# Two-layer-MLP pair behind sparse attention: chunk 0 of the first MLP in program order, eight weight buffers, W_out spilled as one float32 tensor, softmax over eight groups per operation

## The chip, the cores and the metric

The kernel runs on one core of one Trainium2 chip. The metric is the device time of one execution in microseconds (us). Before the change it is 860.85 us, the median of three runs (857.78 to 861.45).

## What is computed

Float64 inputs: q, k, v of shape (4, 8, 576, 64) and four weight matrices. Heads 0 to 3 see a local window of 32 positions, heads 4 to 7 see every 32nd position. The attention output is reshaped to 2304 tokens of 512 and goes through two MLPs with a hidden width of 2048, with different activations.

```python
scores = scale * np.matmul(q, k.transpose(0, 1, 3, 2))
scores = np.where(masks[None, :, :, :], scores, -1000000000.0)
attn = softmax(scores)
x = np.matmul(attn, v)            # then reshaped to (2304, 512)
h = x @ moe_w_in
g = h * np.clip(h + 3.0, 0.0, 6.0) / 6.0
x = g @ moe_w_out
h = x @ moe2_w_in
g = np.maximum(h, 0.0) + np.log1p(np.exp(-np.abs(h)))
return g @ moe2_w_out
```

## The kernel before

**Arithmetic.** Every float32 matrix product is made of three products of a high and a low part (hi x hi, hi x lo, lo x hi; a part is of type fp32r). So a tensor is "split" before TensorE uses it: ScalarE (ACT) copies it to the high part, VectorE (DVE) subtracts that to get the low part. The weights arrive as 64-bit words and are first turned into float32: `w_scale` on ACT changes the upper word in place, then `w_bits` on DVE makes one operation on the lower word (TENSOR_SCALAR, line 121) and one that joins both (SCALAR_TENSOR_TENSOR, line 127).

**Stages.** A prologue computes the attention of the first 96 positions of each batch element, which give chunk 0 (384 tokens). Chunks 1 to 4 are the other 480 tokens of each of the four batch elements. The first MLP walks over chunks, and in each over 16 blocks `f` of 128 hidden columns; one such pair is a *slot*, n = 16 c + f. In a slot TensorE (PE) makes the first product of block f (`pe_h`, 12 matmuls into one of two PSUM banks `psh`) and the second product of the block two slots earlier (`pe_y`, 12 matmuls). Between them stand `post1` (ACT adds 3 and clips, DVE makes the clip at 6 and the product: tile `r`), `post2a` (ACT: high part `gh`) and `post2b` (DVE: low part `gl`). The second MLP follows with its own scheme and is not touched, but its weights are prepared (`prep`) in the slots from chunk 1 on.

**Attention beside the first MLP.** The attention of the tokens of chunk c + 1 is computed in the slots of chunk c. A table `fill`, filled by `put(half-slot, function)`, says in which half-slot each step stands: transposes, `a_qk` (scores into PSUM), `a_max`, `a_exp`, `a_rec`, `a_pt` (transposes), `a_pv`, `a_px`. In `a_max` one fused DVE operation per group of 36 or 64 columns adds the mask and takes the row maximum; `a_exp` is one ACT operation per group, with the sum as an accumulator. There are 16 groups for each kind of head.

**Weights of the first MLP.** In chunk 0 the blocks of W_in and W_out are loaded (512 KB each, DMA issued by SP, five buffers), converted and split. The parts of W_in stay in SBUF for all chunks (`wih`, `wil`). The two parts of W_out (`woh`, `wol`) live in a ring of twelve buffers, are written to DRAM by POOL's queue (`wdr`, two times 256 KB a block) and loaded again four slots ahead in every later chunk (`load_split`).

**Order.** Each engine runs its instructions in the order in which they stand in its program. From chunk 1 on, `in_order` (line 848) makes this the order in which the code is written. In the prologue and in chunk 0 a scheduler in the compiler orders the instructions by its own estimate of when each can start; `after(...)` only keeps some of them behind a few marked ones. The slots of chunk 0 are written in `slot` (line 1244), the prologue is lines 1118 to 1240.

Of the kernel before, what the change touches and what calls it, by code (L numbers as in the profile page):

```python
# [16 lines left out]
P = 128  # L17
# [5 lines left out]
def attn_two_mlps(  # L23
# [51 lines left out]
    ps_a = ctx.enter_context(tc.tile_pool(name="ps_a", bufs=1, space=bass.MemoryType.PSUM))  # L75
# [13 lines left out]
    wdr = [dram.tile([2, P, DM], F32, name=f"wdr{f}") for f in range(NF)]  # L89
# [8 lines left out]
    def load_win(l, f):  # L98
        t = wsl.tile([P, DM], I64, tag="w64", name="wi64", bufs=5)
        nc.sync.dma_start(out=t, in_=w_in[l][f].rearrange("p k f -> p (k f)"))  # L100
        wst_t[0, l, f] = t

    def load_wout(l, f):
        t = wsl.tile([P, DM], I64, tag="w64", name="wo64", bufs=5)
        nc.sync.dma_start(out=t, in_=w_out[l][f * P : (f + 1) * P, :])
        wst_t[1, l, f] = t

# [22 lines left out]

    def split_win(l, f):
        raw = words(0, l, f, F32)[1]
        wst_t.pop((0, l, f))
        hi = wp.tile([P, KT, P], F32R, tag="wih", name="wih")
        lo = wp.tile([P, KT, P], F32R, tag="wil", name="wil")
        wi_t[l, f] = (hi, lo)
# [4 lines left out]
    def sw_tile(name):  # L141
        return sw.tile([P, DM], F32R, tag="sw", name=name)

    def split_wout(f):
        raw = words(1, 0, f, F32)[1]
        wst_t.pop((1, 0, f))
        hi, lo = sw_tile("woh"), sw_tile("wol")
        nc.scalar.copy(hi, raw)
        nc.vector.tensor_tensor(out=lo, in0=raw, in1=hi.bitcast(F32), op=ALU.subtract)
        for i, t in enumerate((hi, lo)):  # L150
            nc.gpsimd.dma_start(out=wdr[f][i], in_=t.bitcast(F32))  # L151
        wo_t[0, f] = (hi, lo)

    def load_split(c, f):
        wo_t[c, f] = tuple(sw_tile(n) for n in ("woh", "wol"))
        for i, t in enumerate(wo_t[c, f]):
            nc.sync.dma_start(out=t.bitcast(F32), in_=wdr[f][i])
# [60 lines left out]
    def prep(k):  # L218
# [7 lines left out]
        if h < 2:  # L226
            w_scale(o, 1, 2 * g + h)
            w_bits((o, 1, 2 * g + h))
# [32 lines left out]
    def ps_two(name):  # L261
        return ps_a.tile([P, 2, 512], F32, tag="a", name=name)

    def ps_att(name):

        x = spare.pop(0)
        if not isinstance(x, tuple):
            return x
        pool, tag = x
        if pool is ps_a:  # L270
            t = ps_two(name)
            spare.insert(0, t[:, 1])
            return t[:, 0]
# [295 lines left out]
    def s_trans(b, n, last=False):  # L569
# [16 lines left out]
        for pr in range(NP):  # L586
# [3 lines left out]
            nc.scalar.copy(u[n + "T"][:, o0 : o0 + end], ps[:, pr, :end])  # L590
# [5 lines left out]
    def a_qk(st, b):  # L596
        ps = ps_two("pss")
        w = KWIN[st]
        for pr in range(NP):
            u = un[st, b, pr]  # L600
            q, k = (u["q"], u["k"]) if st else (u["qT"], u["kT"])
            for g, i, m in blocks(st):
                o = (pr * NG + g) * w
                k0 = (BL if st else w) * m
                for e in range(2):
                    es = slice(e * D, (e + 1) * D)
                    nc.tensor.matmul(
                        ps[i * BL : (i + 1) * BL, e, o : o + w],
# [12 lines left out]
    def a_max(st, b, pr):  # L621

        w = KWIN[st]
        for e in range(2):
            for g in range(NG):
                o = (pr * NG + g) * w
                nc.vector.tensor_tensor_reduce(
                    out=sc_t[st][:, pr, g, e, :w],
                    in0=sc_ps[st, b][:, e, o : o + w],
                    in1=bmask[:, st * KWIN[0] : st * KWIN[0] + w],  # L630
                    scale=-SCALE,
                    scalar=3.0e38,
                    op0=ALU.add,
                    op1=ALU.min,
                    accum_out=stat[st, b][0][:, pr, g, e : e + 1],
                )

    def a_exp(st, b, pr, e):
        nm, sm = stat[st, b]
        for g in range(NG):  # L640
            s = sc_t[st][:, pr, g, e, : KWIN[st]]
            nc.scalar.activation(
                out=s, in_=s, func=AF.Exp, scale=-1.0,
                bias=nm[:, pr, g, e : e + 1], accum_out=sm[:, pr, g, e : e + 1],
            )
# [6 lines left out]
    def a_pt(st, b):  # L652
# [3 lines left out]
        for pr in range(NP):  # L656
            for g in range(NG):
                nc.tensor.transpose(
                    ps[:, pr, g * P : (g + 1) * P],
# [3 lines left out]
        for pr in range(NP):  # L663
            nc.scalar.copy(pt[:, pr], ps[:, pr])
        pt_t[st, b] = pt

    def a_pv(st, b):
# [4 lines left out]
        for pr in range(NP):  # L672
            u = un.pop((st, b, pr))
            for g, i, m in blocks(st):
                for e in range(2):
# [3 lines left out]
                        ps[i * BL : (i + 1) * BL, e, o : o + D],  # L679
# [772 lines left out]
```

## Time and profile before

| | |
|---|---|
| three runs, median (lowest to highest) | 860.85 us (857.78 to 861.45) |
| the profiled execution, its own time | 862.52 us |
| its span in the profile | 860.7 us |
| mean granted TensorE clock in it | 0.989 |
| TensorE matmuls busy | 823.3 us, 96% |
| chunk 0 of the first MLP, first to last matmul of its own | 30.5 to 133.1 us |

How to read it: the profile shows one execution, microsecond by microsecond, from the start of its span. PE is busy nearly all the time, but its busy time counts overlapping, pipelined matmuls, so a stretch in which PE is "busy" is not always one in which it runs at its peak; the start times of its matmuls tell that. Of the 40 slices of the page, PE is below 9 tenths only in the first two, the fifth and the last.

### The profile page before, as it was taken

What the parts mean: (1) busy time and instruction counts of PE and PEld (TensorE: products, weight loads), DVE (VectorE), ACT (ScalarE), POOL (GpSimd) and SP (SyncE); (2) the same over time, 40 slices, a digit from 0 to 9 for tenths busy, and PEclk for the clock granted to TensorE, in tenths of its full rate; (3) what the DMA queues carried; (4) which work ended last, traced back from release to release, by engine and by line L of the source; (5) the groups of instructions that cost most, each with busy time, mean ns of one, the idle gap of its engine ahead of it and who ended that gap; (6) DMA issues with size and microseconds to landing.
All of it is one profiled execution on the core that took longest, in us unless ns stands there. A gap on an engine that the chain in (4) does not pass through costs nothing.

```text
span 860.7 us, 17133 instructions
## 1 busy us (share of the span) xinstructions
PE 823.3 (96%) x6245; PEld 759.9 (88%) x6245; DVE 610.9 (71%) x1231; ACT 484.2 (56%) x978; POOL 80.3 (9%) x133
## 2 busy tenths in 40 slices
PE   4799899999999999999999999999999999999996
PEld 2598888888888888878888899999999999999996
DVE  5596875466865676667677748798677898587784
ACT  4488663564456445664555467853377844478530
POOL 3021121011211112011301100000000000000000
PEclk9799999999999999999999999999999999999998
DMA  8598997499878998776878598777899787997874
GB/s 247 131 381 225 305 324 256 149 205 327 315 270 242 282 297 298 240 237 234 303 269 311 205 353 285 243 249 248 250 289 341 238 249 220 300 306 245 249 247 111
DMA packets 170532, 225.46 MB, mean 262 GB/s; under 512 B 76432, under 2 KB 91664, under 8 KB 170448
## 3 DMA queue, kind: packets, MB, share of 16 engines
q1 hardware_dynamic: 156608, 180.90, 68.4%
q0 software_dynamic: 12032, 42.47, 13.0%
q10 hardware_dynamic: 1808, 0.98, 0.5%
q8 instruction: 50, 0.82, 0.4%
q14 instruction: 34, 0.28, 0.1%
HBM read 177.08 MB, written 47.19 MB: 261 GB/s over the span
## 4 chain that ended last, share of the span: by engine, by line
issue 40%; PE 38%; POOL 7%; DVE 6%; DMA 4%; ACT 4%; SPq 0%; POOLq 0%; DVEq 0%; ACTq 0%
PE psn L1038 15%; PE psm L894 11%; PE psa L1038 6%; POOL sdr L213 5%; PE psh L737 3%; PE psy L781 2%; DVE gq L876 2%; DVE gq L907 2%; DMA wi<-in_w_in_dram 1%; ACT r L913 1%; ACT r L942 1%; ACT r L912 1%; POOL wdr L151 1%; POOL ydr L792 1%; DMA lq<-in_ql_dram 1%
## 5 line engine op out<-in xcount | busy, mean ns | idle before, releaser
L894 PE MATMUL psm<-xh,su 128*128 128x384 f32 x672 | 172.2, 335 | 3.5 <-DVE u L876 3.5
L894 PEld LDWEIGHTS psm<-xh,su 128*128 128x128 f32 x672 | 121.5, 188 | 4.8 <-DVE u L876 4.8
L737 PE MATMUL psh<-xl,wih 128*128 128x480 f32 (+1 forms) x320 | 120.0, 375 | 5.2 <-DVE xl L246 5.2
L1038 PE MATMUL psn<-th,su 128*128 128x384 f32 x480 | 124.6, 339 | 0.0
L781 PE MATMUL psy<-gl,woh 128*128 128x480 f32 (+1 forms) x320 | 119.7, 374 | 3.4 <-DVE gl L764 3.4
L737 PE MATMUL psh<-xh,wih 128*128 128x480 f32 (+1 forms) x320 | 121.3, 379 | 0.6 <-ACT wih L138 0.5
L781 PE MATMUL psy<-gh,wol 128*128 128x480 f32 (+1 forms) x320 | 119.5, 375 | 1.7 <-DVE wi L127 1.7
L781 PE MATMUL psy<-gh,woh 128*128 128x480 f32 (+1 forms) x320 | 119.8, 379 | 0.4 <-ACT gh L758 0.4
L737 PE MATMUL psh<-xh,wil 128*128 128x480 f32 (+1 forms) x320 | 120.0, 375 | 0.0
L894 PE MATMUL psm<-xl,su 128*128 128x384 f32 x336 | 112.3, 334 | 0.0
L969 ACT CAST th<-gq 128x768 fp32r<-128x768 f32 x84 | 68.9, 834 | 69.7 <-PE psn L1038 41.8
L750 ACT ACTIVATE r<-psh 128x480 f32<-128x480 f32 (+1 forms) x80 | 44.6, 557 | 78.0 <-PE psh L737 77.8
L1038 PEld LDWEIGHTS psn<-th,su 128*128 128x128 f32 x480 | 87.5, 188 | 0.0
L758 ACT CAST gh<-r 128x480 fp32r<-128x480 f32 (+1 forms) x80 | 46.2, 578 | 73.3 <-DVE r L751 73.3
L973 DVE TENSOR_TENSOR tl<-gq,th 128x768 fp32r<-128x768 f32 x84 | 77.7, 950 | 8.9 <-ACT th L969 8.9
L1038 PE MATMUL psn<-tl,su 128*128 128x384 f32 x240 | 81.3, 339 | 0.0
L751 DVE SCALAR_TENSOR_TENSOR r<-r,psh 128x480 f32<-128x480 f32 (+1 forms) x80 | 50.3, 630 | 40.9 <-ACT r L750 40.6
L764 DVE TENSOR_TENSOR gl<-r,gh 128x480 fp32r<-128x480 f32 (+1 forms) x80 | 50.6, 634 | 31.8 <-ACT gh L758 31.8
L737 PEld LDWEIGHTS psh<-xl,wih 128*128 128x128 f32 x320 | 61.2, 191 | 12.9 <-DVE xl L246 5.4
L213 POOL DMA_DIRECT2D sdr<-so x64 | 43.5, 681 | 301.5 <-DVE so L212 265.2
L781 PEld LDWEIGHTS psy<-gl,woh 128*128 128x128 f32 x320 | 60.6, 189 | 11.3 <-DVE gl L764 3.6
L737 PEld LDWEIGHTS psh<-xh,wih 128*128 128x128 f32 x320 | 61.0, 191 | 9.4 <-ACT wih L138 1.0
(139 smaller groups left out, 1444.7 us busy)
## 6 DMA issues: line engine op xcount, KB each, us to landing
su<-sdr SPq DMA_DIRECT2D x336, 256.0 KB
sdr<-so POOLq DMA_DIRECT2D x48, 512.0 KB, 5.4
wi<-in_w_in_dram SPq DMA_DIRECT2D x32, 512.0 KB
wo<-in_w_out_dram SPq DMA_DIRECT2D x32, 512.0 KB
woh<-wdr SPq DMA_DIRECT2D x64, 256.0 KB
wol<-wdr SPq DMA_DIRECT2D x64, 256.0 KB
wdr<-woh POOLq DMA_DIRECT2D x16, 256.0 KB, 5.9
wdr<-wol POOLq DMA_DIRECT2D x16, 256.0 KB, 6.4
```

Source lines behind the costliest of these rows:

```text
L213: nc.gpsimd.dma_start(out=sdr[o][g][4 * i + a : 4 * i + z].rearrange("b p n -> p b n"), in_=t.rearrange("p b j n -> p b (j n)").bitcast(F32),)
L737: mark["PE"] = nc.tensor.matmul(ps[:, :n], lhsT=w[:, kt], rhs=x[:, :n], start=(kt == 0 and j == 0), stop=(kt == KT - 1 and j == 2),)
L750: nc.scalar.activation(out=r, in_=ps, func=AF.Relu, bias=3.0)
L751: mark["DVE"] = nc.vector.scalar_tensor_tensor(out=r, in0=r, scalar=6.0, in1=ps, op0=ALU.min, op1=ALU.mult)
L758: mark["ACT"] = nc.scalar.copy(hi, g32_t[l, c, f])
L764: nc.vector.tensor_tensor(out=lo, in0=g32_t.pop((l, c, f)), in1=hi.bitcast(F32), op=ALU.subtract)
L781: mark["PE"] = nc.tensor.matmul(psy_t[l, c][m][:, :w], lhsT=a, rhs=bb, start=(f == 0 and j == 0), stop=(f == NF - 1 and j == 2),)
L876: return nc.vector.tensor_tensor(out=out_, in0=x, in1=y, op=op)
L894: nc.tensor.matmul(ps, lhsT=w[:, kl], rhs=x, start=i in (1, 5, 6) and kl == 0 and j == 0, stop=kl == 1 and j == 2, skip_group_check=True,)
L969: nc.scalar.copy(tt[c, k][0], t_raw(c, k))
L973: nc.vector.tensor_tensor(out=lo, in0=t_raw(c, k), in1=hi.bitcast(F32), op=ALU.subtract)
L1038: nc.tensor.matmul(psl[mt][:, :HT], lhsT=w[:, mt], rhs=x, start=i in (1, 4, 5, 6) and gg == 0 and j == 0, stop=gg == NF2 - 1 and j == 2, s ...
```

## The change

**Chunk 0 in program order.** `in_order` now holds for all slots, so in chunk 0 every engine runs its instructions as `slot` writes them. `slot` writes chunk 0 anew: conversion of W_in block f + 2, the first fill half, `post1` and `post2a`, the split of W_in f + 2, conversion of W_out f, `post2b`, `pe_y`, the second fill half, the split of W_out f.

**Eight weight buffers.** The loads of chunk 0 stand in one list (`order1`) and rotate through the five buffers and three of another pool (`so`, not needed yet). Ten loads are issued before the first slot, two at the end of each slot.

**W_out as float32.** The joining operation (`w_bits`) writes to a tile of the twelve-buffer ring. In chunk 0 this float32 block is written to DRAM once (256 KB). In chunk 1 it is loaded three slots ahead and split again (`split_raw`: an ACT copy and a DVE subtraction in each slot), and the two parts are written to DRAM then; chunks 2 to 4 load the two parts as before.

**Softmax on eight groups.** Per kind of head and per parity `e`, one DVE operation adds the mask for eight groups, one takes the maxima, one subtracts them, one ACT operation makes the exponentials, one DVE operation the sums. The half-slots of these steps move, and `l_load_qk` of the first two batch elements comes three half-slots later. The PSUM tiles of the attention are now two banks in a rotating pair instead of one tile of two banks.

```diff
-    ps_a = ctx.enter_context(tc.tile_pool(name="ps_a", bufs=1, space=bass.MemoryType.PSUM))
+    ps_a = ctx.enter_context(tc.tile_pool(name="ps_a", bufs=2, space=bass.MemoryType.PSUM))
...
+    def w64_tile(name, ring=0):
+        if ring < 5:
+            return wsl.tile([P, DM], I64, tag="w64", name=name, bufs=5)
+        t = wsl.tile([P, 2, 2, DH], F32R, tag="so", name=name, bufs=3)
+        return t.rearrange("p a b n -> p (a b n)").bitcast(I64)
...
+    order1 = [(load_win, 0), (load_win, 1)]
+    for f in range(NF):
+        order1 += [(load_win, f + 2), (load_wout, f)]
+
+    def load_first(k):
+        load, f = order1[k] if k < len(order1) else (None, NF)
+        if f < NF:
+            load(0, f, k % 8)
...
+    def w_bits(o, l, f, out=None):
+        low, _ = words(o, l, f, U32)
+        m, e = words(o, l, f, I32)
+        nc.vector.tensor_scalar(
+            out=m, in0=low, scalar1=2.0**-29, scalar2=7.0, op0=ALU.mult, op1=ALU.min
+        )
+        nc.vector.scalar_tensor_tensor(
+            out=e if out is None else out.bitcast(I32), in0=e, scalar=3, in1=m,
+            op0=ALU.logical_shift_left, op1=ALU.bitwise_or,
+        )
...
+    def wout_split(f):
+        raw, hi, lo = wo_t[0, f]
+        wo_t[0, f] = hi, lo
+        nc.gpsimd.dma_start(out=wdr[f], in_=raw)
         nc.scalar.copy(hi, raw)
-        nc.vector.tensor_tensor(out=lo, in0=raw, in1=hi.bitcast(F32), op=ALU.subtract)
-        for i, t in enumerate((hi, lo)):
-            nc.gpsimd.dma_start(out=wdr[f][i], in_=t.bitcast(F32))
-        wo_t[0, f] = (hi, lo)
+        less(nc.vector, lo, raw, hi)
+
+    def load_raw(c, f):
+        wo_t[c, f] = sw_tile("wol")
+        nc.sync.dma_start(out=wo_t[c, f].bitcast(F32), in_=wdr[f])
+
+    def split_raw(c, f):
+        lo = wo_t[c, f]
+        hi = sw_tile("woh")
+        nc.scalar.copy(hi, lo.bitcast(F32))
+        less(nc.vector, lo, lo, hi)
+        for t, d in zip((hi, lo), wdr2[f]):
+            nc.gpsimd.dma_start(out=d, in_=t.bitcast(F32))
+        wo_t[c, f] = hi, lo
...
+    def a_add(st, b, e):
...
+    def a_max(st, b, e):
+        s, m = sc_view(st, e), stat_view(stat[st, b][0])[:, :, e]
+        nc.vector.tensor_reduce(out=m, in_=s, op=ALU.max, axis=AX)
+        nc.vector.tensor_tensor(
+            out=s, in0=s, in1=m[:, :, None].to_broadcast([P, NP * NG, KWIN[st]]), op=ALU.subtract
+        )
+
+    def a_exp(st, b, e):
+        s = sc_view(st, e)
+        nc.scalar.activation(out=s, in_=s, func=AF.Exp, scale=SCALE)
+
+    def a_sum(st, b, e):
+        nc.vector.reduce_sum(stat_view(stat[st, b][1])[:, :, e], sc_view(st, e), axis=AX)
...
+        for st, qk, pt in ((0, s0 + 4, 13), (1, o + 10, 22)):
             put(qk, a_qk, st, b)
+            for e in range(2):
+                put(qk + 1, a_add, st, b, e)
+                put(qk + 2 + e, a_max, st, b, e)
+                put(qk + 3 + e, a_exp, st, b, e)
+                put(qk + 4 + e, a_sum, st, b, e)
...
             pe_h(l, c, f)
-            if first_use and f + 2 < NF:
-                split_win(0, f + 2)
-            post1(l, c, f)
-            post2a(l, c, f)
...
+            if first_use:
+                if f + 2 < NF:
+                    w_scale(0, 0, f + 2)
+                    win_bits(f + 2)
+            else:
+                post1(l, c, f)
+                post2a(l, c, f)
             if att:
-                for u in fill.get(2 * (NF * c + f), []):
-                    with after(*(["DVE", "PE"] if c == 0 else [])):
-                        u()
+                for u in fill.get(2 * n, []):
+                    u()
+            if first_use:
+                post1(l, c, f)
+                post2a(l, c, f)
+                if f + 2 < NF:
+                    win_split(f + 2)
+                w_scale(1, 0, f)
+                wout_bits(f)
             post2b(l, c, f)
...
             prep(k0 + 1)
-            if n + 4 >= NF and n + 4 < len(seq):
+            if first_use:
+                wout_split(f)
+                load_first(2 * f + 10)
+                load_first(2 * f + 11)
+            if c == 1:
+                split_raw(c, f)
+            if NF <= n + 3 < 2 * NF:
+                load_raw(*seq[n + 3][1:])
+            if 2 * NF <= n + 4 < len(seq):
                 load_split(*seq[n + 4][1:])
...
         for n, step in enumerate(seq):
-            with in_order() if n >= NF else ExitStack():
+            with in_order():
                 slot(n, *step)
```

How instructions move is shown at three places. In the rows, `xl` is the low part of the attention output (MLP input), `wi`/`wo` a loaded 64-bit block, `wir`/`wor` its float32, `wih`/`wil`/`woh`/`wol` the parts, `r`, `gh`, `gl` the tiles of the activation; L121/L127 (now L137/L140) are the two converting operations.

**DVE at the end of the prologue**, before:

```order
L246 TENSOR_TENSOR xl<-psc,xh 128x3x4x32
L121 TENSOR_SCALAR wi_432<-wi_432 128x512
L246 TENSOR_TENSOR xl<-psd,xh 128x192
L127 SCALAR_TENSOR_TENSOR wi_432<-wi_432 128x512
L246 TENSOR_TENSOR xl<-pst,xh 128x3x4x32
```

and now:

```order
L285 TENSOR_TENSOR xl<-pst,xh 128x3x4x32
L285 TENSOR_TENSOR xl<-psd,xh 128x192
L285 TENSOR_TENSOR xl<-pst,xh 128x3x4x32
L146 TENSOR_TENSOR wil<-wir,wih 128x512
L137 TENSOR_SCALAR wi_196<-wi_196 128x512
L285 TENSOR_TENSOR xl<-psd,xh 128x192
L140 SCALAR_TENSOR_TENSOR wir<-wi_196 128x512
L788 SCALAR_TENSOR_TENSOR r<-r,psh 128x384
```

Before, the conversion of `wi_432`, the fifth block of W_in, stands in front of two `xl`; now one `xl` stands behind the conversion of `wi_196`, the third block, whose load is the third of all weight loads.

**DVE in chunk 0**, before (middle of the chunk):

```order
L121 TENSOR_SCALAR wo_1001<-wo_1001 128x512
L764 TENSOR_TENSOR gl<-r,gh 128x384
L139 TENSOR_TENSOR wil<-wi_999,wih 128x512
L751 SCALAR_TENSOR_TENSOR r<-r,psh 128x384
L127 SCALAR_TENSOR_TENSOR wo_1001<-wo_1001 128x512
L751 SCALAR_TENSOR_TENSOR r<-r,psh 128x384
L764 TENSOR_TENSOR gl<-r,gh 128x384
L121 TENSOR_SCALAR wi_1067<-wi_1067 128x512
L149 TENSOR_TENSOR wol<-wo_1001,woh 128x512
```

and now, one slot without fill and the first row of the next:

```order
L788 SCALAR_TENSOR_TENSOR r<-r,psh 128x384
L146 TENSOR_TENSOR wil<-wir,wih 128x512
L137 TENSOR_SCALAR wo_1033<-wo_1033 128x512
L140 SCALAR_TENSOR_TENSOR wor<-wo_1033 128x512
L801 TENSOR_TENSOR gl<-r,gh 128x384
L146 TENSOR_TENSOR wol<-wor,woh 128x512
L137 TENSOR_SCALAR wi_1087<-wi_1087 128x512
L140 SCALAR_TENSOR_TENSOR wir<-wi_1087 128x512
L788 SCALAR_TENSOR_TENSOR r<-r,psh 128x384
```

Before, operations of several blocks are mixed, and the two converting operations of one block stand apart; now they stand together, and each subtraction follows in the slot of its own copy on ACT.

**ACT in chunk 0**, before:

```order
L116 ACTIVATE wo_548<-wo_548 128x512
L590 COPY kT<-psq 128x504 x2
L758 CAST gh<-r 128x384
L138 CAST wih<-wi_546 128x512
L758 CAST gh<-r 128x384
L148 CAST woh<-wo_548 128x512
L116 ACTIVATE wi_607<-wi_607 128x512
```

and now, one slot:

```order
L787 ACTIVATE r<-psh 128x384
L795 CAST gh<-r 128x384
L160 CAST wih<-wir 128x512
L132 ACTIVATE wo_1089<-wo_1089 128x512
L177 CAST woh<-wor 128x512
L132 ACTIVATE wi_1211<-wi_1211 128x512
L787 ACTIVATE r<-psh 128x384
```

Now `wih` of block f + 2 always stands behind `gh` of block f, and `woh` behind both.

## Rows read from the trace of the kernel before

**Rows 1.** The page, busy time, share of the span, instructions

```profile
PE 823.3 (96%) x6245; PEld 759.9 (88%) x6245; DVE 610.9 (71%) x1231; ACT 484.2 (56%) x978; POOL 80.3 (9%) x133
```

**Rows 2.** Engines by stretch: busy us (instructions), granted clock, DMA share, GB/s

```profile
30.00:40.00 10.00, 4.29 (x13) 2.87 (x13) 4.72 (x12) 4.09 (x9) 0.00 (x0) 0.65 0.58 119
40.00:50.00 10.00, 9.97 (x53) 9.67 (x53) 9.20 (x19) 8.43 (x17) 2.54 (x4) 0.83 0.92 323
...
80.00:90.00 10.00, 6.65 (x150) 6.03 (x149) 4.88 (x9) 6.00 (x13) 1.09 (x2) 0.88 0.97 250
90.00:100.00 10.00, 9.35 (x54) 9.06 (x54) 8.17 (x18) 5.87 (x11) 2.16 (x4) 0.94 1.11 314
...
133.00:210.00 77.00, 76.78 (x852) 65.64 (x851) 41.06 (x128) 37.34 (x113) 7.61 (x12) 1.00 0.75 222
```

**Rows 3.** Timeline of PE: start us, us, instructions, [idle before <- releaser]

```profile
30.47 0.44 PE L737 MATMUL psh<-xh,wih 128*128 128x384 f32 x1
36.09 0.69 PE L737 MATMUL psh<-xl,wih 128*128 128x384 f32 x1 [5.18 <-DVE xl L246]
...
70.50 0.34 PE L737 MATMUL psh<-xh,wih 128*128 128x384 f32 x1
...
74.70 0.34 PE L737 MATMUL psh<-xh,wih 128*128 128x384 f32 x1
...
87.28 0.44 PE L781 MATMUL psy<-gl,woh 128*128 128x384 f32 x1 [3.35 <-DVE gl L764]
...
88.08 0.53 PE L781 MATMUL psy<-gl,woh 128*128 128x384 f32 x1
...
123.54 0.38 PE L737 MATMUL psh<-xh,wih 128*128 128x480 f32 x1
```

**Rows 4.** Timeline of DVE, chunk 0

```profile
35.34 0.43 DVE L121 TENSOR_SCALAR wi<-wi 128x512 int32<-128x512 uint32 x1 [5.20 <-DMA wi<-in_w_in_dram]
...
55.84 0.42 DVE L121 TENSOR_SCALAR wi<-wi 128x512 int32<-128x512 uint32 x1
56.36 0.69 DVE L127 SCALAR_TENSOR_TENSOR wi<-wi 128x512 int32<-128x512 int32 x1
56.97 0.42 DVE L121 TENSOR_SCALAR wo<-wo 128x512 int32<-128x512 uint32 x1
...
62.73 0.18 DVE L627 CUSTOM_DVE_ANT_0 sc<-pss,bmask 128x36 f32<-128x36 f32 x1
...
64.57 0.68 DVE L127 SCALAR_TENSOR_TENSOR wo<-wo 128x512 int32<-128x512 int32 x1
...
86.33 0.43 DVE L121 TENSOR_SCALAR wo<-wo 128x512 int32<-128x512 uint32 x1 [4.73 <-DMA wo<-in_w_out_dram]
...
93.74 1.28 DVE L688 TENSOR_TENSOR xn<-pso,sm 128x512 f32<-128x512 f32 x2
...
100.86 1.08 DVE L246 TENSOR_TENSOR xl<-psx,xh 128x480 fp32r<-128x480 f32 x1
...
104.05 0.55 DVE L751 SCALAR_TENSOR_TENSOR r<-r,psh 128x384 f32<-128x384 f32 x1
```

**Rows 5.** Timeline of ACT, chunk 0

```profile
104.63 0.51 ACT L758 CAST gh<-r 128x384 fp32r<-128x384 f32 x1 [0.70 <-DVE r L751]
...
107.65 0.51 ACT L758 CAST gh<-r 128x384 fp32r<-128x384 f32 x1 [0.83 <-DVE r L751]
108.07 1.07 ACT L664 COPY pt<-psp 128x512 f32<-128x512 f32 x2
```

**Rows 6.** Groups by line, 30 to 133 us: count, busy us, mean ns, idle before

```profile
L148 ACT CAST woh<-wo 128x512 fp32r<-128x512 f32 x16 | 10.7, 672 | 5.5 <-DVE wo L127 5.4
...
L138 ACT CAST wih<-wi 128x512 fp32r<-128x512 f32 x15 | 9.8, 666 | 2.4 <-DVE wi L127 2.2
```

**Rows 7.** Timeline of SP's queue, chunk 1: DMA issues

```profile
174.51 5.07 SPq L550 DMA_DIRECT2D vl<-in_vl_dram  x4
...
192.93 0.57 SPq L157 DMA_DIRECT2D woh<-wdr  x1
```

More of the change, by code (lines that the diff above doesn't have):

```diff
@@ L137, in split_win, with less, win_bits, win_split @@
+    def less(eng, lo, raw, hi):
+        eng.tensor_tensor(
+            out=lo, in0=raw.bitcast(F32), in1=hi.bitcast(F32), op=ALU.subtract
+        )
+    def win_bits(f):
+        wi_t[0, f] = sw_tile("wir", F32)
+        w_bits(0, 0, f, wi_t[0, f])
+        wst_t.pop((0, 0, f))
+    def win_split(f):
+        raw = wi_t[0, f]
+        hi, lo = (wp.tile([P, KT, P], F32R, tag=f"wi{n}", name=f"wi{n}") for n in "hl")
+        wi_t[0, f] = (hi, lo)
         hi, lo = (t.rearrange("p k f -> p (k f)") for t in (hi, lo))
@@ L138, in split_win, with sw_tile, wout_bits @@
         nc.scalar.copy(hi, raw)
-        nc.vector.tensor_tensor(out=lo, in0=raw, in1=hi.bitcast(F32), op=ALU.subtract)
[L141 to L145, printed above, removed]
+        less(nc.vector, lo, raw, hi)
+    def sw_tile(name, dt=F32R):
+        return sw.tile([P, DM], dt, tag="sw", name=name)
+    def wout_bits(f):
+        wo_t[0, f] = tuple(
+            sw_tile(n, dt) for n, dt in (("wor", F32), ("woh", F32R), ("wol", F32R))
+        )
+        w_bits(1, 0, f, wo_t[0, f][0])
@@ L146, in split_wout @@
         wst_t.pop((1, 0, f))
-        hi, lo = sw_tile("woh"), sw_tile("wol")
+    def wout_split(f):
+        raw, hi, lo = wo_t[0, f]
+        wo_t[0, f] = hi, lo
+        nc.gpsimd.dma_start(out=wdr[f], in_=raw)
         nc.scalar.copy(hi, raw)
-        nc.vector.tensor_tensor(out=lo, in0=raw, in1=hi.bitcast(F32), op=ALU.subtract)
-        for i, t in enumerate((hi, lo)):
-            nc.gpsimd.dma_start(out=wdr[f][i], in_=t.bitcast(F32))
-        wo_t[0, f] = (hi, lo)
+        less(nc.vector, lo, raw, hi)
@@ L261, in ps_two @@
     def ps_two(name):
-        return ps_a.tile([P, 2, 512], F32, tag="a", name=name)
+        return [ps_a.tile([P, 512], F32, tag="a", name=name) for _ in range(2)]
     def ps_att(name):
[L266 to L273, printed above, removed]
+        pool, tag = spare.pop(0)
         return pool.tile([P, 512], F32, tag=tag, name=name)
@@ L589, in s_trans @@
                 u[n + "T"] = st_tile(n + "T")
-            nc.scalar.copy(u[n + "T"][:, o0 : o0 + end], ps[:, pr, :end])
+            nc.scalar.copy(u[n + "T"][:, o0 : o0 + end], ps[pr][:, :end])
     def blocks(st):
@@ L619, in attn_two_mlps, with sc_view, stat_view @@
     sc_ps, stat, pt_t, xn_t = {}, {}, {}, {}
[L621 to L645, printed above, removed]
+    def sc_view(st, e):
+        return sc_t[st].rearrange("p r g e k -> p (r g) e k")[:, :, e, : KWIN[st]]
+    def stat_view(t):
+        return t.rearrange("p r g e -> p (r g) e")
+    def a_add(st, b, e):
+        w, n = KWIN[st], NP * NG
+        mk = bmask[:, st * KWIN[0] : st * KWIN[0] + w]
+        nc.vector.tensor_tensor(
+            out=sc_view(st, e),
+            in0=sc_ps[st, b][e][:, : n * w].rearrange("p (n k) -> p n k", k=w),
+            in1=mk[:, None, :].to_broadcast([P, n, w]),
+            op=ALU.add,
+        )
+    def a_max(st, b, e):
+        s, m = sc_view(st, e), stat_view(stat[st, b][0])[:, :, e]
+        nc.vector.tensor_reduce(out=m, in_=s, op=ALU.max, axis=AX)
+        nc.vector.tensor_tensor(
+            out=s, in0=s, in1=m[:, :, None].to_broadcast([P, NP * NG, KWIN[st]]), op=ALU.subtract
+        )
+    def a_exp(st, b, e):
[3 more added lines that the diff above has]
+        nc.vector.reduce_sum(stat_view(stat[st, b][1])[:, :, e], sc_view(st, e), axis=AX)
     def a_rec(st, b):
@@ L663, in a_pt @@
         for pr in range(NP):
-            nc.scalar.copy(pt[:, pr], ps[:, pr])
+            nc.scalar.copy(pt[:, pr], ps[pr])
         pt_t[st, b] = pt
@@ L1018, in pe2 @@
                 a = ps_two("psa")
-                bank[1] = [a[:, 0], a[:, 1]]
+                bank[1] = a
             elif i in (5, 6, 4):
@@ L1235, in attn_two_mlps @@
             s_load_v(0, pr)
+        for k in range(5, 10):
+            load_first(k)
         with after("xh", "xl"):
-            w_scale(1, 0, 0)
-            split_win(0, 1)
-            w_scale(0, 0, 2)
-            w_bits((0, 0, 2))
+            win_split(1)
         seq = [(0, c, f) for c in range(NC1) for f in range(NF)]
@@ L1280, in slot @@
                 pe_y(*seq[n - 2])
-            if first_use and f + 1 < NF:
-                w_scale(1, 0, f + 1)
             if att:
-                for u in fill.get(2 * (NF * c + f) + 1, []):
-                    with after(*(["DVE", "PE"] if c == 0 else [])):
-                        u()
+                for u in fill.get(2 * n + 1, []):
+                    u()
             prep(k0 + 1)
-            if n + 4 >= NF and n + 4 < len(seq):
+            if first_use:
[7 more added lines that the diff above has]
+            if 2 * NF <= n + 4 < len(seq):
                 load_split(*seq[n + 4][1:])
```

108 lines of the change are left out of this document (35 added, 73 removed).

## The prediction

> **What bounds the kernel now.** I read the page first: TensorE (PE) is busy 96% of the span, VectorE (DVE) 71%, ScalarE (ACT) 56% [rows 1]. So the change can only matter where PE does not run. The table by stretches finds the place: from 133 us to 210 us PE is busy 76.78 of 77 us at full clock, but in chunk 0 there are stretches such as 30 to 40 and 80 to 90 us with 4.29 and 6.65 of 10 us, and a granted clock of 0.65 and 0.88 [rows 2]. PE's timeline names the two holes: 5.18 us until a low part `xl` is there, and 3.35 us until a `gl` is there [rows 3]. DVE's timeline shows what is behind them: both times DVE itself sat still in front of a weight block that had not landed, for 5.20 us and 4.73 us [rows 4], with the wanted `xl` and `gl` queued behind it. The order of chunk 0 put a conversion too early. Where nothing is late, a slot takes 4.20 us on PE (two starts of `pe_h`, 70.50 and 74.70) [rows 3].
>
> What could be won at most: the two holes, 8.5 us, the time lost to the low clock, which by the granted clock is about 1.5 (4.29 us at 0.65) + 1.7 + 0.8 + 0.6 = 4.6 us in the four 10 us stretches [rows 2], and a few small holes: 14 to 16 us.
>
> **The new order, step by step.** In the new chunk 0 DVE's order in a slot is r, wil, the two conversions of W_out, gl, wol, the two conversions of W_in, and ACT's is relu, gh, wih, scale, woh, scale. Both engines take one instruction after another, so the slot has a closed chain that passes from one to the other and back twice. From `r` of one slot to `r` of the next:
>
> - r on DVE 0.55, and 0.03 until ACT starts gh (104.05 + 0.55 = 104.60, start 104.63) [rows 4, 5];
> - gh until ACT can start the next one 0.42 (107.65 to 108.07) [rows 5]; wih 0.67 [rows 6]; 0.03 back to DVE;
> - wil until the next start 0.61 (as 56.36 to 56.97), first conversion until the dependent second 0.52 (55.84 to 56.36), second 0.69 [rows 4];
> - 0.03 to ACT, woh 0.67 [rows 6], 0.03 to DVE; gl runs beside it;
> - wol 0.61, first conversion 0.52, second until r starts 0.61 [rows 4].
>
> Together 5.99; without rounding, 5.9 to 6.0 us. I take 5.95. That is 1.75 us more than PE needs for the slot. DVE waits 1.2 us of it before wil (for gh and wih), 0.3 before wol, and 0.4 in the dependent pairs. Nothing hides this: the next `r` is behind it, and `pe_h` needs the PSUM bank that `r` frees, `pe_y` needs gl and wol. The scale operations on ACT lie in ACT's own waits and cost nothing; if they grew by over 0.6 us they would delay relu.
>
> **Start of the chain.** The conversion that blocked DVE until 35.34 now belongs to the third block in the queue, loaded long before, so the 5.18 us hole goes. PE is ready at 30.47 [rows 3]. Then ACT still makes two high parts, wih (0.67) and a scale, DVE the last `xl`: about 2.5 us. Eight matmuls follow (1.4 us at full, up to 2.8 at the low clock) and relu: the first r at 35.2 to 36.5 us; I take 35.2.
>
> **Attention of the first batch element, on the chain.** The mask-add, maximum, subtraction and sum are each two DVE operations of 288 columns for strided heads, 512 for local ones. The trace has none of these; the nearest are 512 columns in 0.64 (1.28 for two) [rows 4] and 384 columns in 0.55. By columns I get 0.36 and 0.64, so 8 x 0.36 + 8 x 0.62 = 7.9 us. The lower bound is what the replaced operations took, since the new ones pass over the same columns and more often: 16 fused operations of the strided heads 1.84 us (62.73 to 64.57) [rows 4], about 4 us for both kinds. I take 7.9, the nearer row in size. To that come reciprocals and dependent pairs (0.7, estimated from the 0.1 us of a pair), four xn (2.6), and two strided xl (2.1) [rows 4]: 13.3 us. Some 1.3 of it falls into the 0.3 us holes before wol. So 12 us up to slot 13; bounds 8 and 14.
>
> The Trainium skill, page "VectorE: DVE Perf Modes", section "Rules for kernel authors", says to keep the number of operations small. By it, halving the operations should make the softmax cheaper on DVE, at an estimate 1 us per kind of head instead of 3 to 5, and the sum would be some 6 us smaller. The row speaks against it here: a fused operation of 36 columns costs 0.115 us, so there is little fixed cost to save, and the new form passes over the columns four times instead of once.
>
> **End of chunk 0.** r of slot 13 starts at 35.2 + 13 x 5.95 + 12 = 124.5. Its wol comes 4.9 us later by the same steps, then ten matmuls of `pe_y` at 0.175 (4.20 / 24) end at 131.2. Slots 14 and 15 have no W_in work, so from there PE sets the pace. In the trace of before PE reaches this point, the first matmul of 480 columns, at 123.54 [rows 3]. Chunk 0 gets **7.6 us longer**: the chain takes back all of the 15 us and more.
>
> **Chunks 1 to 4.** Re-splitting adds 0.6 us DVE and 0.6 us ACT a slot in chunk 1; with DVE at 41 and ACT at 37 of 77 us [rows 2] PE covers it. If that cover failed, it would cost at most 16 x 0.6 = 10 us. The 4 us more DVE softmax per batch element is hidden the same way. One wait is new: ACT's copy in slot n needs a block loaded three slots earlier, and behind SP's queue of small transfers (174.51 to 192.93, 18.4 us) [rows 7] the block for slot 28 is issued late. relu and gh of the next slot stand behind it on ACT, but PE has up to a slot in hand. I take 1 us, bounds 0 and 5. The eight buffers and the halved writes of chunk 0 cost and gain nothing by themselves: at 6 us a slot the 1.3 MB (two loads, one write) are 220 GB/s, less than the 323 moved at 40 to 50 us [rows 2].
>
> **Sum.** 862.5 + 7.6 + 1.0 = 871.1 us for an execution like the profiled one, which lies 1.7 above the median: **869.4 us**. Bounds of this case: first r +1.3, crossings and pairs -0.2 to +0.2 per slot (3 us), attention -4 to +2, chunk 1 -1 to +4: 862 to 878.
>
> **Rivals.**
>
> *Faster: the chain is not closed.* If DVE and ACT in effect overlap two slots, by whatever means, PE bounds chunk 0 and the 14 to 16 us come in: 862.5 - 15 - 1.7 = 846 us. For it: DVE's pure work in a slot is 4 us, below 4.20, both holes of rows 3 vanish, and the softmax leaves ACT. Against: the printed order leaves no row between gh and wih or between woh and wol to overlap. It decides if a slot takes under 5 us. Chance 0.18.
>
> *About even.* Chain at its lower bound and attention mostly in the holes: 856 to 862, between the cases. Chance 0.10.
>
> *Slower still: the clock falls.* After the 3.35 us hole PE's matmuls took 0.53 instead of 0.34 us (88.08) [rows 3], the lower of the two levels, 1.2 instead of 2.4 GHz; in 30 to 40 us the same after 5.18 us. With PE idle in nearly a third of each slot, and for 3 us in the slots that carry attention, this could come again. At the low level a slot needs up to 8.4 us on PE, 2.4 above the chain; over four to eight slots that is 10 to 20 us: 879 to 889. Against: the holes of a plain slot are at most 1.2 us, and a PE that is slow becomes the bound, has no holes any more and gets its clock back, as by 100 us. Chance 0.12.
>
> The Trainium skill, page "TensorE: Matmul & The Clock Gate", section "HAM oscillation — how this bites in real kernels", describes a loop whose waits bring the array back to the low level in every round. By it this case would be the likeliest; the rows show the fall only behind the two longest holes, so I leave it at a small chance.
>
> *The change does not do what it says:* weights might land no earlier than before. They would then stop DVE as at 86.33 (4.73 us) [rows 4]; 874, inside my range.
>
> **How the numbers follow.** The forecast case has 0.60 (862 to 878), of which 0.05 below 865.2. A difference under 0.5% (4.3 us) can't be told from no change here: 856.5 to 865.2. Faster: 0.18 and 0.02 of the even case, 0.20. Same: 0.08 + 0.05 = 0.13. Slower: 0.55 + 0.12 = 0.67. The range takes the forecast's, the even case's and half of the clock's: 853 to 884. It leaves out most of the fast case.
>
> **What would show it.** Right: starts of `pe_h` 5.9 us apart in slots without attention; DVE's waits led by wil on wih and wol on woh; no DVE wait on weight loads; the first 480-column matmul near 131. The start: no wait of 5 us at 30 us. The softmax: its eight operations in 3 and 5 us. Wrong: slots of 4.2 to 5 us (the chain overlaps), matmuls of 0.5 us (the clock), or holes of PE after 140 us (chunk 1).

## The result, and the profile after

The changed kernel takes 865.86 us (median of five runs, 864.04 to 866.64), the kernel before in the same comparison 858.79 us: a ratio of 1.0070, 95% interval 1.0047 to 1.0093. A second comparison (`a0_after` below) gave 864.71 against 860.17 us, 1.0055 (1.0037 to 1.0074). So the change makes the kernel **slower, by 0.4 to 0.9%**; the prediction said 869.4 us and slower. The two profiled executions lie closer together (864.04 and 862.52 us): the one of before was slow for its kernel, the one of after fast.

The page's busy line, beside [rows 1]:

```profile
PE 823.7 (96%) x6245; PEld 755.0 (88%) x6245; DVE 637.2 (74%) x1055; ACT 457.3 (53%) x754; POOL 88.4 (10%) x149
```

Engines by stretch after, columns as in [rows 2]:

```profile
30.00:40.00 10.00, 7.08 (x43) 6.68 (x43) 5.73 (x11) 5.58 (x11) 0.72 (x1) 0.95 1.02 261
40.00:50.00 10.00, 10.00 (x173) 9.61 (x172) 7.92 (x15) 6.63 (x15) 1.09 (x2) 0.88 1.02 399
...
80.00:90.00 10.00, 8.13 (x44) 6.54 (x42) 7.55 (x16) 4.24 (x9) 0.55 (x1) 1.00 0.69 208
90.00:100.00 10.00, 8.30 (x40) 6.41 (x40) 8.40 (x15) 6.99 (x12) 1.08 (x2) 1.00 0.81 166
...
133.00:210.00 77.00, 77.00 (x853) 66.26 (x852) 54.60 (x95) 36.43 (x68) 20.97 (x37) 1.00 0.85 257
```

The hole at the start has gone (7.08 instead of 4.29 us of PE in 30 to 40), but in 80 to 100 us PE is busy 16.4 of 20 us, as before (16.0), and no engine is full: DVE has 16, ACT 11 of 20 us. That is how two engines look that wait for each other in turn. DVE's timeline of one slot without attention shows it:

```profile
44.38 0.55 DVE L788 SCALAR_TENSOR_TENSOR r<-r,psh 128x384 f32<-128x384 f32 x1
46.03 0.69 DVE L146 TENSOR_TENSOR wil<-wir,wih 128x512 fp32r<-128x512 f32 x1 [1.10 <-ACT wih L160]
46.64 0.42 DVE L137 TENSOR_SCALAR wo<-wo 128x512 int32<-128x512 uint32 x1
47.17 0.69 DVE L140 SCALAR_TENSOR_TENSOR wor<-wo 128x512 int32<-128x512 int32 x1
47.78 0.55 DVE L801 TENSOR_TENSOR gl<-r,gh 128x384 fp32r<-128x384 f32 x1
48.55 0.69 DVE L146 TENSOR_TENSOR wol<-wor,woh 128x512 fp32r<-128x512 f32 x1 [0.22 <-ACT woh L177]
49.16 0.42 DVE L137 TENSOR_SCALAR wi<-wi 128x512 int32<-128x512 uint32 x1
49.68 0.69 DVE L140 SCALAR_TENSOR_TENSOR wir<-wi 128x512 int32<-128x512 int32 x1
50.29 0.55 DVE L788 SCALAR_TENSOR_TENSOR r<-r,psh 128x384 f32<-128x384 f32 x1
```

and ACT's timeline of the same slot:

```profile
44.97 0.51 ACT L795 CAST gh<-r 128x384 fp32r<-128x384 f32 x1 [1.16 <-DVE r L788]
45.39 0.61 ACT L160 CAST wih<-wir 128x512 fp32r<-128x512 f32 x1
45.91 0.68 ACT L132 ACTIVATE wo<-wo 128x512 f32<-128x512 f32 x1
47.90 0.62 ACT L177 CAST woh<-wor 128x512 fp32r<-128x512 f32 x1 [1.31 <-DVE wor L140]
48.42 0.68 ACT L132 ACTIVATE wi<-wi 128x512 f32<-128x512 f32 x1
49.00 0.47 ACT L787 ACTIVATE r<-psh 128x384 f32<-128x384 f32 x1
```

From the start of one `r` to that of the next it is 50.29 - 44.38 = 5.91 us, of which DVE waits 1.10 + 0.22 and ACT 1.16 + 1.31 us. The waits of DVE, 30 to 133 us (us in total, times, longest), name no weight load any more, and no row of PE; the first two:

```profile
DVE wil L146 <- ACT wih L160: 15.4, 14, 1.1
DVE wol L146 <- ACT woh L177: 1.7, 8, 0.2
```

The chain of waits at the end of chunk 0 goes through the same hands (start us, us):

```profile
123.28 0.70 DVE wor L140
...
124.00 0.63 ACT woh L177
...
124.66 0.70 DVE wol L146
...
125.40 2.02 PE psy L818 x10
```

PE's timeline, beside [rows 3]: it starts 3 us earlier, has two long holes, with matmuls of 0.52 us behind each, and reaches the first matmul of 480 columns at 127.26 instead of 123.54. Both holes stand in front of rows of attention; as DVE waits for no row of PE, they do not lengthen the chain.

```profile
27.51 0.43 PE L774 MATMUL psh<-xh,wih 128*128 128x384 f32 x1
...
37.62 1.14 PE L612 MATMUL psq<-ident,sk 126*128 126x126 f32 x8 [2.81 <-ACT qT L622]
...
39.23 0.52 PE L774 MATMUL psh<-xh,wih 128*128 128x384 f32 x1
...
69.35 1.62 PE L695 MATMUL psp<-ident,sc 128*128 128x128 f32 x8 [4.34 <-DVE sc L663]
...
71.09 0.52 PE L774 MATMUL psh<-xl,wih 128*128 128x384 f32 x1
...
127.26 0.38 PE L774 MATMUL psh<-xh,wih 128*128 128x480 f32 x1
```

Behind chunk 0 the profiled execution gains again. The waits of PE after 120 us, leaving out one of 0.4 us before and one of 0.5 us after, were before:

```profile
PE psm L894 <- DVE u L876: 3.5, 4, 1.7
PE psp L658 <- DVE xl L246: 2.1, 3, 1.5
```

and after:

```profile
PE psm L931 <- DVE u L913: 1.8, 3, 0.7
PE psh L774 <- issue: 1.1, 1, 1.1
```

That is 5.6 against 2.9 us, about what the 3.7 us at 127.26 shrink by to the 1.5 us between the two spans (862.2 and 860.7). The kernel before was profiled once, so where the rest of the difference between the medians lies cannot be seen.

### The profile page after: what moved, and what is told of

Read it like the earlier page. It is cut to its first block, busy times and chain, and to the rows that moved or that the text cites. A ratio compares the mean times of both kernels' runs of the same rounds, so it can differ in the third digit from the quotient of the medians.

```text
span 862.2 us, 16753 instructions
## 1 busy us (share of the span) xinstructions
PE 823.7 (96%) x6245; PEld 755.0 (88%) x6245; DVE 637.2 (74%) x1055; ACT 457.3 (53%) x754; POOL 88.4 (10%) x149
## 4 chain that ended last, share of the span: by engine, by line
PE 54%; issue 16%; DVE 5%; ACT 4%; POOL 3%; DMA 2%; POOLq 0%; SPq 0%; DVEq 0%; ACTq 0%
PE psn L1075 15%; PE psm L931 11%; PE psy L818 10%; PE psh L774 10%; PE psa L1075 6%; POOL sdr L252 2%; DVE gq L913 2%; DVE gq L944 2%; ACT r L950 1%; DMA su<-sdr 1%; ACT r L979 1%; ACT r L949 1%; PE pso L715 1%; DVE u L913 1%; PE pss L639 1%
## 5 line engine op out<-in xcount | busy, mean ns | idle before, releaser
L774 PEld LDWEIGHTS psh<-xh,wil 128*128 128x128 f32 x320 | 60.8, 190 | 10.1 <-DVE wil L146 2.6
L818 PEld LDWEIGHTS psy<-gh,wol 128*128 128x128 f32 x320 | 60.0, 188 | 10.6 <-DVE wol L146 2.4
```

What stands on the lines that cost most here:

```text
L774: mark["PE"] = nc.tensor.matmul(ps[:, :n], lhsT=w[:, kt], rhs=x[:, :n], start=(kt == 0 and j == 0), stop=(kt == KT - 1 and j == 2),)
L818: mark["PE"] = nc.tensor.matmul(psy_t[l, c][m][:, :w], lhsT=a, rhs=bb, start=(f == 0 and j == 0), stop=(f == NF - 1 and j == 2),)
```

## Experiments

The theory: chunk 0 is set by the closed chain DVE, ACT, DVE, ACT of a slot, and this comes from the order in which the slot is written alone. Ratios are to the kernel before on the same chip. The diffs are cut to the lines that matter; the conditions for the last blocks are left out.

### The order: undone, and mended

**e1_sched**: the scheduler orders chunk 0 again (and `after(...)` stands around the fill steps as before).

```diff
-            with in_order():
+            with in_order() if n >= NF else ExitStack():
                 slot(n, *step)
```

> The changed kernel with the program order of chunk 0 alone undone: the scheduler orders chunk 0 again; the buffers, the float32 W_out and the softmax stay. Theory (the closed chain of DVE and ACT, 5.90 us a slot, is what chunk 0 costs): slots of 4.2 to 5 us where nothing is late; what is left are stalls in front of a conversion whose block has not landed, since the scheduler again puts conversions early. With stalls of 0 to 10 us in all: 846 to 860 us. Rival (softmax and the new split cost the time, not the order): 864 to 868, the same as the changed kernel.

Measured: 848.89 us, 0.9864 (0.9850 to 0.9877). All the rest of the change, in the scheduler's order, wins 1.4%; program order as written takes 2% back. The stall in front of a weight block is still there, once: DVE's and PE's timelines have

```profile
37.42 0.43 DVE L137 TENSOR_SCALAR wo<-wo 128x512 int32<-128x512 uint32 x1 [4.39 <-DMA wo<-in_w_out_dram]
```

```profile
38.50 0.69 PE L774 MATMUL psh<-xh,wil 128*128 128x384 f32 x1 [4.53 <-DVE wil L146]
```

and after it PE is busy 10.00 us of every 10 (here DVE too, so nothing waits in turn):

```profile
60.00:70.00 10.00, 10.00 (x178) 9.65 (x177) 10.00 (x22) 6.73 (x13) 1.09 (x2) 1.00 1.05 332
```

**e2_order**: program order stays; three lines of the slot move (`win_split` now makes ACT's copy and returns DVE's subtraction).

```diff
+                w_scale(1, 0, f)
                 post1(l, c, f)
+                win_lo = win_split(f + 2)
                 post2a(l, c, f)
-                win_split(f + 2)
-                w_scale(1, 0, f)
                 wout_bits(f)
+                win_lo()
```

> The changed kernel with three lines of the slot of chunk 0 moved: ACT's copy wih stands between relu and gh (its input is there already), the scale of W_out before relu, and DVE's subtraction wil behind the two conversions of W_out. The same instructions, in another order. Theory (closed chain): no row of DVE waits for ACT any more, so a slot is DVE's own work, 0.55 + 0.52 + 0.61 + 0.61 + 0.47 + 0.61 + 0.52 + 0.61 = 4.50 us instead of 5.90. r of slot 13 comes 13 x 1.4 = 18 us earlier, at 102, with attention still 11.4 us on DVE; time 866 - 18 = 848. Rival 1 (weights): chunk 0 moves some 24.6 MB, in 85 instead of 103 us that is 290 GB/s; if the loads don't come that fast, DVE waits for them and 5 to 10 us are won: 856 to 861. Rival 2 (the order of these rows does not matter; softmax, clock or PE set chunk 0): 864 to 868.

Measured: 847.62 us, 0.9847 (0.9834 to 0.9861): as the theory says, and the shortest median of the study. The same instructions, the same computation, **some 18 us less** than the changed kernel. The three moves were not tried one by one. DVE's timeline of a slot has no wait left, and lasts 46.34 - 42.00 = 4.34 us:

```profile
42.00 0.55 DVE L788 SCALAR_TENSOR_TENSOR r<-r,psh 128x384 f32<-128x384 f32 x1
...
43.53 0.69 DVE L146 TENSOR_TENSOR wil<-wir,wih 128x512 fp32r<-128x512 f32 x1
...
44.60 0.69 DVE L146 TENSOR_TENSOR wol<-wor,woh 128x512 fp32r<-128x512 f32 x1
...
46.34 0.55 DVE L788 SCALAR_TENSOR_TENSOR r<-r,psh 128x384 f32<-128x384 f32 x1
```

PE reaches the first matmul of 480 columns 17.1 us earlier than in the changed kernel:

```profile
110.12 0.38 PE L774 MATMUL psh<-xh,wih 128*128 128x480 f32 x1
```

**e5_order2**: on top of e2_order, the two conversions of one block stand apart, W_in's a slot earlier (`w_low` is the first operation of `w_bits`, which then makes the second only).

```diff
-                w_scale(0, 0, f + 2)
-                win_bits(f + 2)
...
                 w_scale(1, 0, f)
+                w_scale(0, 0, f + 3)
                 post1(l, c, f)
                 win_lo = win_split(f + 2)
                 post2a(l, c, f)
+                w_low(1, 0, f)
+                w_low(0, 0, f + 3)
                 wout_bits(f)
+                win_bits(f + 3)
                 win_lo()
```

> The kernel with the three moved lines, and the two conversions of one block set apart: first operation of W_out f, first of W_in f + 3, then the second of each. Theory (a slot is DVE's own work, and the pair on one block costs some 0.1 to 0.2 us each): from the rows of the kernel with the moved lines, 0.47 + 0.34 + 0.34 + 0.61 + 0.61 + 0.60 + 0.47 + 0.61 = 4.05 us, below PE's 4.20, so PE sets plain slots at 4.20 instead of 4.36; 13 x 0.16 = 2 us: 845.5, or 0.982 of before. Rival (attention, not the plain slot, sets what is left): 847 to 848.5, as with the moved lines alone.

Measured: 850.64 us, 0.9883 (0.9857 to 0.9909): a miss, slower than with the three lines alone. DVE's work did fall to 4.0 us a slot, but ACT's timeline shows what I had set in front of relu in the second slot:

```profile
36.55 0.65 ACT L132 ACTIVATE wo<-wo 128x512 f32<-128x512 f32 x1 [2.58 <-DMA wo<-in_w_out_dram]
38.12 0.65 ACT L132 ACTIVATE wi<-wi 128x512 f32<-128x512 f32 x1 [0.92 <-DMA wi<-in_w_in_dram]
38.68 0.47 ACT L791 ACTIVATE r<-psh 128x384 f32<-128x384 f32 x1
```

ACT stood 3.5 us, and r 4.6 us, in front of these blocks. The one needed a slot too early is W_in's, at 38.12; so r of this slot starts at 39.18, in e2_order at 37.62. It is the fault of the kernel before, in a new place, and it has a second part: PE had a hole of 4.03 us, and behind it matmuls of 0.52 us, the lower of the two levels (granted clock 0.50 from 40 to 45 us, where e2_order has 1.00).

**e11_order3**: the pairs apart without needing a block earlier; the diff is against e2_order.

```diff
                 w_scale(0, 0, f + 2)
-                win_bits(f + 2)
+                w_low(0, 0, f + 2)
...
                 w_scale(1, 0, f)
                 post1(l, c, f)
-                win_lo = win_split(f + 2)
                 post2a(l, c, f)
+                w_low(1, 0, f)
+                win_bits(f + 2)
+                win_lo = win_split(f + 2)
                 wout_bits(f)
-                win_lo()
             post2b(l, c, f)
+            win_lo()
```

> The kernel with the two conversions of one block set apart, in a form that needs no block earlier: the first operation of W_in f + 2 in front of r, then r, the first of W_out f, the second of W_in, the second of W_out, gl, wil, wol; ACT: both scales before relu, gh, wih, woh. By the rows of the last runs 0.34 + 0.47 + 0.34 + 0.61 + 0.61 + 0.47 + 0.60 + 0.61 = 4.05 us on DVE. Theory (the 4.5 us hole in the second slot, where ACT's scale stood before relu and waited for a block that was needed a slot earlier, is all that spoiled the last form): no such hole, plain slots at PE's 4.20, 0.982 to 0.984 of before (845 to 847 us). Rival (something else in that order costs it, the kT wait of 4.0 us or attention): 0.986 or more.

Measured: 848.41 us, 0.9848 (0.9822 to 0.9873). The hole is gone, but the time is that of e2_order, between the two numbers expected. Plain slots are 4.23 to 4.34 us, the first 480-column matmul comes at 109.73. The pairs were not what is left. In e2_order's chain of waits DVE is followed back only up to 91 us; from there on PE carries it:

```profile
90.42 0.61 DVE wil L146
91.08 2.01 PE psh L774 x10
```

### The other parts, each undone alone

**a0_after** is the changed kernel again.

> The changed kernel itself once more, to compare the others with it on one chip. 864 to 867 us, 1.003 to 1.008 of before.

Measured: 864.71 us, 1.0055 (1.0037 to 1.0074).

**Buffers.** e6_ring5 is the changed kernel, e7_sched_ring5 is e1_sched, e10_order_ring5 is e2_order, each with five buffers:

```diff
-            load(0, f, k % 8)
+            load(0, f, k % 5)
```

> The changed kernel with five instead of eight weight buffers for chunk 0. Theory (closed chain): at 5.9 us a slot 1 MB of weights in a slot is some 180 GB/s, so five buffers are enough, and the time is that of the changed kernel within 1.5 us. Rival (the buffers carry the change): DVE or ACT wait for weight loads again, 3 us or more longer.

> The scheduler's order in chunk 0 with five buffers; the softmax and the float32 W_out stay as changed. Against the run with the scheduler's order and eight buffers (0.9864 of before) it says what the buffers are worth when slots are short. Theory 1 (stalls on weights were what held the kernel before, and the buffers take them away): the stalls come back, 5 to 9 us, 0.992 to 0.997 of before. Theory 2 (the softmax and the single write of W_out took them away): within 2 us of that run, 0.984 to 0.989.

> The kernel with the three moved lines, with five instead of eight weight buffers. In the changed kernel five buffers cost nothing, though its PE then waited 6.9 us for a k block of the local heads and 2.8 us for a v block, whose loads stand in SP's queue behind weight loads that wait for a buffer. Theory (those waits fell into the slack of the closed chain; with slots of 4.36 us there is none left): 3 to 8 us longer than with eight buffers, 0.988 to 0.994 of before, with PE waiting for the k and v loads. Rival (five buffers are enough at 4.36 us too): 0.983 to 0.986.

Measured: e6_ring5 865.85 us, 1.0058 (1.0035 to 1.0080); e7_sched_ring5 853.09 us, 0.9909 (0.9885 to 0.9932); e10_order_ring5 855.88 us, 0.9935 (0.9909 to 0.9960). In the closed chain five buffers cost nothing that can be told from noise (a0_after, on the same chip, has 864.71 us); in the scheduler's order they cost 0.45%, between the two theories, in the mended order 0.9%. In e7_sched_ring5 the weight blocks themselves come late, with a longest wait of 5.9 us where e1_sched has 4.39:

```profile
DVE wo L137 <- DMA wo<-in_w_out_dram: 7.0, 2, 5.9
```

In the other two the first to suffer are small loads in SP's queue behind weight loads that wait for a buffer. PE's waits in e6_ring5:

```profile
PE pss L639 <- DMA lk<-in_kl_dram: 6.9, 2, 6.6
PE pso L715 <- DMA vl<-in_vl_dram: 2.8, 3, 2.3
```

and in e10_order_ring5:

```profile
PE pss L639 <- DMA lk<-in_kl_dram: 6.0, 2, 5.2
PE pso L715 <- DMA vl<-in_vl_dram: 1.5, 2, 1.2
```

Nearly the same waits, about 1 us by the medians in one, within its noise, and 8 in the other. In e6_ring5 PE had the wait for k to spare while DVE and ACT set the pace: r of slot 13 starts at 120.19, in the changed kernel at 120.51. In e10_order_ring5 the 6.0 us are not all: behind them PE's matmuls take 0.52 us for a while, and the granted clock of the stretch is 0.68, where e2_order has 1.00:

```profile
60.00:70.00 10.00, 9.21 (x129) 8.83 (x115) 6.14 (x14) 2.39 (x6) 0.36 (x1) 0.68 0.57 201
```

The first matmul of 480 columns comes at 118.76, 8.6 us later than in e2_order.

**Softmax.** e3_fused is the changed kernel, e8_sched_fused is e1_sched, with `a_max` and `a_exp` of before in place of `a_add`, `a_max`, `a_exp`, `a_sum`, in the half-slots of before.

> The changed kernel with the softmax of before (one fused DVE operation a group, one exponential a group on ACT), the rest as changed. Theory (closed chain): DVE loses 8.8 us of softmax and gets back some 4; ACT gets 32 exponentials with their accumulators, 16.3 us in the trace of before, instead of 2.2. In a closed chain ACT's work counts too, as far as it does not fit into its own waits (2.8 us a slot): the time is 862 to 872, and the slots that carry exponentials are longer. Rival (the softmax's DVE work alone makes the loss): 866 - 5 = 861 or less.

> The scheduler's order in chunk 0, eight buffers and the float32 W_out, with the softmax of before. In the run with the scheduler's order DVE was busy all the time from 50 to 100 us, ACT 38 of 50 us. Theory 1 (DVE sets this stretch): 4 to 5 us of softmax less on DVE, 0.981 to 0.984 of before. Theory 2 (the 14 us of exponentials more on ACT fill its room): no gain, 0.986 to 0.993. If 2 holds, the wide softmax is a part that wins time under the scheduler's order and costs some in the closed chain.

Measured: 860.16 us, 0.9995 (0.9984 to 1.0005), against 1.0055 for the changed kernel (another chip); and 852.74 us, 0.9900 (0.9873 to 0.9927), against 0.9864. So in the closed chain the wide softmax loses 0.6%: the theory for e3_fused was wrong, and its rival's number (861 or less) was met. With the fused softmax the same chain takes the time of the kernel before; so the loss against it goes with either part undone, and the order is the larger one, 18 us against 5. In the scheduler's order the wide softmax wins some 0.4%, as the second theory had it; but the intervals just touch, the six runs of e8_sched_fused spread from 849.23 to 854.20 us, and its profiled execution (849.23) lies 0.5 us from that of e1_sched, so no trace shows where the gain lies. ACT's added work in e3_fused (count, busy us, mean ns) was

```profile
L674 ACT ACTIVATION_READ_ACCUMULATOR sc<-sc,nm 128x1 f32 x32 | 6.1, 190 | 0.0
L674 ACT ACTIVATE sc<-sc,nm 128x64 f32<-128x64 f32 x16 | 5.3, 339 | 0.0
L674 ACT ACTIVATE sc<-sc,nm 128x36 f32<-128x36 f32 x16 | 4.9, 312 | 0.0
```

16.3 us where the wide form has 2.2. Nearly all of it went into ACT's own waits; only twice did exponentials in front of relu hold up r, by 0.41 and 0.45 us. On DVE, from start to next start, the 32 fused operations took 4.1 us and the 16 wide ones 8.2. r of slot 13 came at 118.82, so attention took (118.82 - 33.08) - 13 x 5.92 = 8.8 us of the chain instead of 11.4. As the first r came 0.7 us later, r of slot 13 is 1.7 us earlier than in the changed kernel, and the profiled executions lie 2.2 us apart (861.79 and 864.04); the rest of the 5 us between the medians is not located.

**W_out.** e4_parts is the changed kernel, e9_sched_parts is e1_sched, with the parts written in chunk 0, loaded from chunk 1 on, and no second split (only the first of these is shown):

```diff
-        nc.gpsimd.dma_start(out=wdr[f], in_=raw)
         nc.scalar.copy(hi, raw)
         less(nc.vector, lo, raw, hi)
+        for t, d in zip((hi, lo), wdr2[f]):
+            nc.gpsimd.dma_start(out=d, in_=t.bitcast(F32))
```

> The changed kernel with W_out handled as before: both parts written in chunk 0 and loaded in chunks 1 to 4, no second split. Theory (the float32 W_out costs and wins nothing): within 1.5 us of the changed kernel, 864 to 867; slots of chunk 0 still 5.90, PE without holes in chunk 1 either way. Rival 1 (the second split costs time in chunk 1): 860 to 863. Rival 2 (the doubled writes slow the loads of chunk 0): 869 or more, with DVE or ACT waiting for weight loads.

> The scheduler's order in chunk 0, eight buffers and the wide softmax, with W_out's two parts written in chunk 0 as before. The DMA engines' mean share was 1.00 to 1.10 from 30 to 90 us in the run with the single write. Theory 1 (DMA is full there, 256 KB more a slot come out of the weight loads): 16 x 256 KB = 4.2 MB at some 330 GB/s are 12 us of DMA time, of which 2 to 7 reach the end, 0.989 to 0.995 of before. Theory 2 (the writes find room): 0.985 to 0.988.

Measured: 863.55 us, 1.0042 (1.0029 to 1.0056), between theory and rival 1 and the same as the changed kernel within the intervals; and 852.51 us, 0.9900 (0.9874 to 0.9925), against 0.9864, as the first theory had it. The single write is worth nothing in the closed chain and some 0.4% (again with intervals that touch) where slots are short. That full DMA engines are the cause is not shown: their share from 30 to 80 us is no higher in the profile of e9_sched_parts (0.88 to 1.05) than in that of e1_sched (1.00 to 1.05).

Buffers, softmax and single write are worth 0.45, 0.36 and 0.36% in the scheduler's order, 1.2% together if they add up, which no run tests, of the 1.36% that e1_sched wins as a whole. The moved half-slots, the rotating pair of PSUM banks and the new order of the prologue were not undone.

## Why the prediction was right

- **The closed chain, 5.95 us a slot: right.** Measured 5.90, with DVE's waits of 1.10 and 0.22 us where 1.2 and 0.3 were named. e2_order shows that this is the cause, and e1_sched that the order alone brings it.
- **The start, first r at 35.2: too late by 2.8 us.** It took PE's 30.47 from the trace of before as given. The last parts of x came earlier: DVE made the first of them for tile `pst` at 27.00, and PE began at 27.51. The prologue had been ordered anew too; which of its changes did it was not tried.
- **Attention, 12 us on the chain: measured 11.4**, (120.51 - 32.39) - 13 x 5.90. The durations were taken rightly from rows of 384 and 512 columns: two mask-adds took 0.81 and 1.28 us, for 0.72 and 1.24. The Trainium skill, page "VectorE: DVE Perf Modes", section "Rules for kernel authors", counts operations; by that the wide form should have cost less on DVE. The measurement decides against it here: 16 wide operations took 8.2 us of DVE and held the chain 2.6 us longer than 32 fused ones, which took 4.1. What the wide form saves is on ACT.
- **The end of chunk 0, +7.6 us: measured +3.7** in the profiled execution; nearly all of the difference is the start and 13 x 0.05 us.
- **Chunks 1 to 4, +1.0 us: not seen.** PE has 77.00 of 77 us in 133 to 210; later there is one hole of 1.1 us that no wait explains. The profiled execution gained 2.2 us behind chunk 0, mostly in the second MLP's waits.
- **The sum: its direction right, its size in part luck.** Against the median of before +8.5 us was forecast; +7.1 and +4.5 were measured. Term by term the traces give less: +3.7 at the end of chunk 0 and -2.2 behind it, +1.5 us between the two profiled executions, where 871.1 against 862.5 was forecast. The medians lie nearer to the forecast than the traces do, and no trace shows why. (The bounds named for the sum add up to over 879 at the top, not 878; nothing hangs on it.)
- **The rival "the chain is not closed", 846 us:** the price was right, the condition was not met. e2_order meets it, with slots under 5 us, and takes 847.62 us. Its plain slots are DVE's work and not PE's: with the dependent pairs that work is 4.34 us, not the 4 us that the rival counts.
- **The rival "the clock falls":** it fell twice in the profiled execution, behind the holes of 2.81 and 4.34 us, where matmuls took 0.52 us, the lower of the two levels, for some 3 us each. In the profile of a0_after it fell behind the second only (4.40 us). It cost nothing, since no row of DVE waits for PE in chunk 0. The slots of 80 to 100 us, with PE idle 18% of the time in short holes, ran at a granted clock of 1.00. The Trainium skill, page "TensorE: Matmul & The Clock Gate", section "HAM oscillation — how this bites in real kernels", tells of a loop whose waits bring the low level back in every round; this loop's waits did not, so the small chance was right. The waits in that section's example are several times as long as the holes of up to 0.8 us here, so it did not make this case the likeliest, as the prediction has it.
- **Eight buffers cost and gain nothing: right** in this kernel, and only in it.

## What to carry to other kernels

When two engines pass work back and forth, put the rows in an order in which each copy is made one step before its subtraction is due: the same instructions took 5.9 or 4.34 us a slot. Look for it where neither engine is full and PE waits a little in every round. And a part that measures as worth nothing, or less, may only be hidden behind such a chain: once the chain was gone, the buffers became worth 0.45 to 0.9%, and the single write and the softmax perhaps 0.4% each. Moving an operation forward is safe only if its data are there by then.

## What was not expected

Some 14 us more work on ACT in chunk 0 held up r by under 1 us (e3_fused), since ACT's waits for DVE took in nearly all of it. And a wait of PE of 6 to 7 us for one small load left the closed chain where it was (e6_ring5), while the same wait, of 6.0 us, together with the low clock behind it, was most of 8 us in the mended order (e10_order_ring5).
